# Attention, a dense and a routed MoE layer on one core: late scores with both query parts stacked on the rows

## The chip, the cores and the metric

The kernel runs on one core of a Trainium2 chip. The metric is the device time of one execution in microseconds (us). Before the change, three runs took 986.07, 986.64 and 989.24 us; the median is 986.64.

## The reference

Inputs are fp32. Attention has batch 4, 8 heads, 576 positions and head size 64; the mask works on blocks of 64 positions, so that query block i (0 to 8) sees key blocks 0 to i. Its output feeds a dense layer with a maximum over three products, and that feeds a routed layer with 8 experts, of which each of the 2304 tokens uses 2.

```
scores = scale * q @ k.T ; scores = where(block_i >= block_j, scores, -1e9)
attn = exp(scores - max) ; attn /= attn.sum(-1) + 1e-9 ; out = attn @ v
x = out in rows of 512 (8 heads x 64)
x = max(x @ w1, x @ w2, x @ w3) @ w_out
logits = x @ w_gate + log1p(exp(x @ w_noise)) * noise ; top 2, softmax
out[t] = sum over its 2 experts of weight * (relu(x[t] @ e1[e]) @ e2[e])
```

## The kernel before

**Jobs.** A job is two heads of one batch, and either the early query blocks 0 to 3 or the late ones 4 to 8. There are 32 jobs, 16 of them late. The first eight (early, of batches 0 and 1) run in `start`, whose order for all engines is planned from written costs, due times and dependencies (`add(engine, cost, ...)`) and kept. The other 24 run in a loop behind it, in the order of `MIDDLE`, written by hand: one late job, three early, two late and so on, with ten late jobs in a row at the end. Ten times a late job directly follows a late one. There the scheduler of the tile framework orders each engine's instructions by its own simulation, with the program's order as priority; what the engines execute is that order.

**Between the jobs' steps** the loop calls `gap(j)`, which adds 1.0 us (1.2 us from job 16 on) to a budget and lets the generator `chain` emit as much of the dense layer: units of 256 tokens, in groups of 24 products of 256 columns (L811 to L813), then products of 264 columns (L836 to L840) and the routing (L931 and on). After attention, the rest of the dense layer and the routed layer follow (from 440 us on).

**A late job, exactness.** The scores use fp32r products of a high and a low part: Qh Kh + Ql Kh + Qh Kl. `split_keys` (L284) makes Kh on ScalarE (L288) and Kl = k - Kh on GpSimd (L291), `split_queries` (L293) makes Qh on ScalarE (L298) and Ql on VectorE (L300). The two heads lie on partitions 0 to 63 and 64 to 127. The stationary operand of one query block is block diagonal (128x128, `late_queries` L229 clears the rest), so that one product over 128 rows gives 64 queries of both heads. `prep_job` (L302) does all four for the next late job, right after the scores of the late job before it, since Kh, Kl, Qh and Ql have one buffer each. `load_job` (L271) has by then brought the raw tiles rq and rk, also one buffer each, through SP's queue; the next job's load is issued behind `prep_job`.

**Scores** (`s_block`, L329): for block i, three products with 64 i + 64 columns (L313, L314, L315; block 8 has two halves of 288 columns in tile a2) into one of two PSUM tiles `s`; a maximum on VectorE (L319), an exponential with a row sum on ScalarE (L320) into the tile `PL[i]`, and `scale` (L392: add, reciprocal, multiply on VectorE). `turn_steps` and `score_steps` (L1028 to L1041) pair the transposes of job j with the scores of job j + 1, and a gap stands behind each of five steps:

```
turns  (j):     4 and tail of 8 | 8 | 6 | 7 | 5
scores (j + 1): 4 | 8, scale(4, 8) | 6 | 7, scale(6, 7) | 5, scale(5)
```

**Transposes** (`t_block`, L404; L402) go to PSUM tiles `t` and from there on ScalarE (L416) into the weights tile `PT[j]`, which uses the buffers Ph and Pl in turn. **Values** (`pv`, called behind the scores of the next job): ten fp32 products (L467), a pair for each of five key steps, one head on columns 0 to 63 and one on 64 to 127 of the array. An fp32 product has two records in the trace.

**Memory.** The first eight jobs use four sets of buffers, three of which lie in Qh, Kh, Ph, Ql, Kl, Pl and V. The tiles `PL` also serve the gate's small products in `start` (L569 to L582), by their numbers.

Of the kernel before, what the change touches and what calls it, by code (L numbers as in the profile page):

```python
# [129 lines left out]
def tile_attention_moe_moe(ctx, tc, qT, kT, v, w1, w2, w3, w_out, gates, noise, e1, e2, out):  # L130
    nc = tc.nc
# [70 lines left out]
    PL = {i: att.tile([128, 384 if i == 5 else 128 * (i // 2 + 1)], F32, name=f"p{i}") for i in range(4, 9)}  # L202
    POFF = {3: 0, 2: 256, 0: 512, 1: 640}
    SLOT = {8: 0, 6: 1, 7: 2, 4: 3, 5: 4}

    jp = PL[5][:, :128]
# [11 lines left out]
    LT = {x: n for x, n in (("Qh", 640), ("Ql", 640), ("Kh", S), ("Kl", S), ("V", 1280), ("Ph", 2560), ("Pl", 2560))}  # L218
    t = {x: att.tile([128, n], F32, name=x) for x, n in LT.items()}
    new_set(t["Qh"][:, :512], t["Kh"][:, :512], t["Ph"][:, :768], t["Ph"][:, 768:1536])  # L220
    new_set(t["Ql"][:, :512], t["Kl"][:, :512], t["Ph"][:, 1536:2304], t["Pl"][:, :768])
    new_set(t["V"][:, :512], t["V"][:, 512:1024], t["Pl"][:, 768:1536], t["Pl"][:, 1536:2304])
# [6 lines left out]
    def late_queries(n):  # L229
        QQ.append(att.tile([128, 5, 128], F32R, name=("Qh", "Ql")[n]))  # L230
        nc.gpsimd.memset(plain(QQ[n]), 0.0)

    def late_tails():
        for i in (4, 6, 8):
            nc.gpsimd.memset(PL[i][:, 64 * i + 64:], 0.0)

# [34 lines left out]
    def load_job(j):  # L271
        i = at(j)
        q = att.tile([128, 320], F32, name="rq")
        k = att.tile([128, S], F32, name="rk")
        nc.sync.dma_start(q, qT[i:i + 2, :, 256:S].rearrange("h d n -> (h d) n"))
        nc.sync.dma_start(k, kT[i:i + 2].rearrange("h d n -> (h d) n"))
        RAW[j] = q, k

    def load_values(j):
        n = LJ.index(j) % 2  # L280
        VV[j] = att.tile([128, 1280 if n else 640], F32, name=("rv", "V")[n])[:, :640].rearrange("p (r c) -> p r c", r=2)
        nc.sync.dma_start(VV[j], v[at(j):at(j) + 2].rearrange("h p c d -> p h (c d)"))

    def split_keys(j, low):  # L284
        k = RAW[j][1]
        if not low:
            QK[j] = (att.tile([128, S], F32R, name="Kh"),)
            nc.scalar.activation(QK[j][0], k, AF.Copy)  # L288
        else:
            QK[j] += (att.tile([128, S], F32R, name="Kl"),)  # L290
            nc.gpsimd.tensor_sub(QK[j][1], k, plain(QK[j][0]))  # L291

    def split_queries(j, r, low):  # L293
        m = slice(64 * r, 64 * r + 64)
        src = RAW[j][0][m].rearrange("p (i c) -> p i c", c=64)
        h, l = (x[m, :, m] for x in QQ)
        if not low:
            nc.scalar.activation(h, src, AF.Copy, scale=0.125)  # L298
        else:
            nc.vector.scalar_tensor_tensor(l, src, 0.125, plain(h), op0=OP.mult, op1=OP.subtract)  # L300
# [9 lines left out]
    def scores(ps, j, i, k0, k1):  # L310
        Kh, Kl = QK[j]
        QH, QL = (x[:, i - 4] for x in QQ)
        nc.tensor.matmul(ps, QH, Kh[:, k0:k1], start=True, stop=False)  # L313
        nc.tensor.matmul(ps, QL, Kh[:, k0:k1], start=False, stop=False)  # L314
        nc.tensor.matmul(ps, QH, Kl[:, k0:k1], start=False, stop=True)  # L315
# [11 lines left out]
    SB = {}  # L327

    def s_block(j, i, c):  # L329
        st = new_stats(j)  # L330
        if i == 8:
            ps = psA[0].tile([128, 2, 512], F32, name="a2")
            for r in range(2):
                scores(ps[:, r, 0:288], j, i, 288 * r, 288 * r + 288)
            exps(st, c, ps[:, :, 0:288], PL[8][:, :576].rearrange("p (a b) -> p a b", a=2))
            return
        SB[i] = bank("s")
        ps = SB[i][:, :64 * i + 64]
        scores(ps, j, i, 0, 64 * i + 64)
        exps(st, c, ps, PL[i][:, :64 * i + 64])  # L340

# [50 lines left out]
    def scale(j, c0, blocks):  # L392
        st, z = ST[j][:, 1, c0:c0 + len(blocks)], SB[blocks[0]][:, 500:500 + len(blocks)]
        nc.vector.tensor_scalar(z, st, 1.0e-9, None, op0=OP.add)
        nc.vector.reciprocal(st, z)
        for c, i in enumerate(blocks):
            s = ST[j][:, 1, c0 + c:c0 + c + 1]
            P = PL[i][:, :64 * i + 64]
            nc.vector.tensor_scalar(P, P, s, None, op0=OP.mult)

# [3 lines left out]
    def t_block(j, i, tail=None):  # L404
        if j not in PT:
            PT[j] = att.tile([128, 2, 4, 320], F32, name=("Ph", "Pl")[LJ.index(j) % 2])
        nk = (i + 2) // 2
        if i == 8:
            nk = 4
        ps = bank("t")  # L410
        for key in range(nk):
            turn(ps[:, 128 * key:128 * key + 128], i, key)
        if tail is not None:
            turn(ps[:, 384:512], tail, 4)
        o = 64 * SLOT[i]
        nc.scalar.activation(PT[j][:, :, :nk, o:o + 64].rearrange("p h k c -> p k h c"),  # L416
                             ps[:, :128 * nk].rearrange("p (k h c) -> p k h c", k=nk, h=2), AF.Copy)
        if tail is not None:
# [140 lines left out]
    GT = PL[5][:, 128:192].rearrange("p (k n) -> p k n", k=4)  # L559
# [8 lines left out]
    def gate_copy(g, c):  # L568
        nc.scalar.activation(PL[7 + c][:, :512], GS[g, c], AF.Copy)  # L569
# [888 lines left out]
```

## Time and profile before

| what | us |
|---|---|
| median of three runs | 986.64 |
| the profiled execution | 986.13 |
| its span, from the first to the last instruction | 984.4 |
| PE busy (matmuls) | 971.0 |
| VectorE (DVE) busy | 431.2 |
| ScalarE (ACT) busy | 395.5 |
| GpSimd (POOL) busy | 392.6 |

PE is TensorE. The line numbers are those of the kernel before. A matmul's row gives its start and its duration; matmuls are pipelined, so that the distance from one start to the next is what a product costs PE. "128*64" is the stationary operand: rows by columns of the array. `x20` behind a row says that 20 instructions in a row are merged into it. What ended an idle time is inferred from semaphores.

### The profile page before, as it was taken

Reading aid. Unit: us, or ns where it says so; the run is one execution under the profiler, and the core shown is the slowest. Engines: PE = TensorE matmul, PEld = TensorE weight load, DVE = VectorE, ACT = ScalarE, POOL = GpSimd, SP = SyncE. Lnnn points to the kernel's source line nnn. Section 1 sums busy time; section 2 is a strip of 40 time slices with the busy share of each in tenths; the row PEclk is TensorE's granted clock in tenths of the full one; section 3 lists DMA queues with packets and bytes.
Section 4 is the critical chain, followed back from the end, with each engine's and each line's share of the span. In section 5 each row is a group of like instructions: output and inputs, shape, how many; then the busy total and the mean of one; then the engine's idle time right before and its main releaser. Section 6 shows DMA issues by size and latency. Waiting matters only on the chain. (4 is left out here: it accounts for less than half of the span.)

```text
span 984.4 us, 17147 instructions
## 1 busy us (share of the span) xinstructions
PE 971.0 (99%) x6594; PEld 861.2 (87%) x6594; DVE 431.2 (44%) x1259; ACT 395.5 (40%) x938; POOL 392.6 (40%) x298
## 2 busy tenths in 40 slices
PE   9999999999999999999999999999999999999997
PEld 5856899999898998999999889898988979898895
DVE  7854657654677665632355322222222222221321
ACT  7587545544565555531134234142323323132210
POOL 3595121211213013120221577755836556564302
PEclk9999999999999999999999999999999999999999
DMA  9912414221211312212022546543535354452101
GB/s 322 340 29 71 134 47 155 54 90 31 62 55 36 92 36 68 63 30 85 22 81 82 173 160 196 180 151 108 184 108 162 109 155 146 126 170 77 52 14 57
DMA packets 72550, 106.17 MB, mean 108 GB/s; under 512 B 19196, under 2 KB 44796, under 8 KB 72464
## 3 DMA queue, kind: packets, MB, share of 16 engines
q1 hardware_dynamic: 61120, 75.93, 24.1%
q0 software_dynamic: 10224, 28.32, 8.8%
q8 instruction: 53, 0.87, 0.4%
q10 hardware_dynamic: 1120, 0.79, 0.3%
q14 instruction: 33, 0.27, 0.1%
HBM read 85.35 MB, written 20.53 MB: 108 GB/s over the span
## 5 line engine op out<-in xcount | busy, mean ns | idle before, releaser
L187 POOL TENSOR_TENSOR w<-rw,w 128x1536 fp32r<-128x1536 f32 (+1 forms) x42 | 131.7, 3137 | 71.7 <-ACT w L186 56.2
L827 POOL TENSOR_TENSOR hl<-hm,hh 128x512 fp32r<-128x512 f32 x21 | 27.7, 1317 | 173.3 <-ACT hh L826 173.2
L186 ACT ACTIVATE w<-rw 128x1536 fp32r<-128x1536 f32 (+1 forms) x42 | 56.5, 1345 | 89.2 <-issue 42.1
L1179 PE MATMUL b<-xh,w 128*128 128x384 f32 (+7 forms) x272 | 87.4, 322 | 0.7 <-DVE xB L1184 0.4
L1180 PE MATMUL b<-xl,w 128*128 128x384 f32 (+7 forms) x272 | 87.4, 321 | 0.3 <-DVE xl L1170 0.3
L1181 PE MATMUL b<-xh,w 128*128 128x384 f32 (+7 forms) x272 | 87.6, 322 | 0.0
L811 PE MATMUL t<-xA,w 128*128 128x256 f32 x288 | 83.1, 289 | 0.0
L812 PE MATMUL t<-xA,w 128*128 128x256 f32 x288 | 81.7, 284 | 0.0
L813 PE MATMUL t<-xA,w 128*128 128x256 f32 x288 | 81.5, 283 | 0.0
L1184 DVE SCALAR_TENSOR_TENSOR ht<-b,ht 128x384 fp32r<-128x384 f32 (+6 forms) x56 | 29.1, 520 | 94.3 <-ACT ht L1183 94.3
L1235 POOL DMA_INDIRECT out_rows<-y,isc x37 | 37.5, 1013 | 77.3 <-DVE y L1232 73.1
L1180 PE MATMUL t<-xl,w 128*128 128x256 f32 x240 | 67.3, 280 | 0.0
L1181 PE MATMUL t<-xh,w 128*128 128x256 f32 x240 | 67.3, 280 | 0.0
L1179 PE MATMUL t<-xh,w 128*128 128x256 f32 x240 | 67.3, 281 | 0.0
L1227 PE MATMUL b<-w,ht 128*128 128x512 f32 (+1 forms) x168 | 67.0, 399 | 0.0
L291 POOL TENSOR_TENSOR Kl<-rk,Kh 128x576 fp32r<-128x576 f32 x16 | 23.2, 1450 | 109.0 <-ACT Kh L288 109.0
L1229 PE MATMUL b<-w,ht 128*128 128x512 f32 (+1 forms) x168 | 66.4, 395 | 0.0
L1228 PE MATMUL b<-w,ht 128*128 128x512 f32 (+1 forms) x168 | 66.3, 394 | 0.0
L999 POOL DMA_INDIRECT ids<-rows,slots x36 | 35.9, 996 | 68.4 <-DVE slots L996 60.1
L811 PE MATMUL t<-xB,w 128*128 128x256 f32 x216 | 61.9, 287 | 0.0
L812 PE MATMUL t<-xB,w 128*128 128x256 f32 x216 | 61.3, 284 | 0.0
L813 PE MATMUL t<-xB,w 128*128 128x256 f32 x216 | 61.2, 283 | 0.0
(404 smaller groups left out, 2766.7 us busy)
## 6 DMA issues: line engine op xcount, KB each, us to landing
rw<-in_e SPq DMA_DIRECT2D x32, 768.0 KB, 4.6
w<-in_w SPq DMA_DIRECT2D x18, 512.0 KB, 7.8
rw<-in_e SPq DMA_DIRECT2D x16, 512.0 KB, 3.7
rk<-in_kT SPq DMA_DIRECT2D x16, 288.0 KB, 2.8
x2d<-x SPq DMA_DIRECT2D x18, 256.0 KB, 2.0
out_rows<-x SPq DMA_DIRECT2D x9, 512.0 KB, 3.0
w<-in_w_out SPq DMA_DIRECT2D x6, 512.0 KB, 10.1
rq<-in_qT SPq DMA_DIRECT2D x16, 160.0 KB, 2.3
```

What stands on the lines that cost most here:

```text
L186: nc.scalar.activation(t[:, 0, :c], r[:, :c], AF.Copy)
L187: nc.gpsimd.tensor_sub(t[:, 1, :c], r[:, :c], plain(t[:, 0, :c]))
L811: nc.tensor.matmul(ps[:, j], wh, x[:, 0], start=kt == 0, stop=False)
L812: nc.tensor.matmul(ps[:, j], wh, x[:, 1], start=False, stop=False)
L813: nc.tensor.matmul(ps[:, j], wl, x[:, 0], start=False, stop=kt == 3)
L1179: nc.tensor.matmul(p, wt1(e, 0, kt, f), th[:, kt, c0:c1], start=kt == 0, stop=False)
L1180: nc.tensor.matmul(p, wt1(e, 0, kt, f), tl[:, kt, c0:c1], start=False, stop=False)
L1181: nc.tensor.matmul(p, wt1(e, 1, kt, f), th[:, kt, c0:c1], start=False, stop=kt == 3)
L1227: nc.tensor.matmul(ps, a, wt2(e, 0, f), start=f == 0, stop=False)
L1228: nc.tensor.matmul(ps, a, wt2(e, 1, f), start=False, stop=False)
L1229: nc.tensor.matmul(ps, l, wt2(e, 0, f), start=False, stop=f == 7)
L1235: st = nc.gpsimd.indirect_dma_start(out=out, out_offset=bass.IndirectOffsetOnAxis(ap=at, axis=0), in_=y, in_offset=None, bounds_check=NTOK ...
```

## The change

The late queries are laid out per head. For head r, one operand holds the high part on one half of the rows and the low part on the other (`QQ[r]`), and Kh lies on both halves, so that one product over 128 rows gives Qh Kh + Ql Kh of one head for 128 queries: blocks 4 and 5, or 6 and 7, together. Qh Kl of a head is a product over the 64 rows of the high part. The even block of a pair gets 64 columns of keys too many; they are set to -1e9 in PSUM before the maximum. Block 8 stays one product group for both heads, with the operands padded by zeros and a block-diagonal copy of its high part that GpSimd makes (`block_queries`). A pair takes both `s` tiles, one for each head. The raw queries and keys are loaded on both halves (four DMAs a job instead of two). Scores and transposes have new steps; the weights use Ph alone, and every second job's values lie in Pl.

```diff
-    LT = {x: n for x, n in (("Qh", 640), ("Ql", 640), ("Kh", S), ("Kl", S), ("V", 1280), ("Ph", 2560), ("Pl", 2560))}
+    LT = {x: n for x, n in (("Qh", 512), ("Ql", 384), ("Kh", 2 * S), ("Kl", S), ("V", 768), ("Ph", 2560), ("Pl", 2304))}
...
+        q = att.tile([128, (512, 384)[n]], F32R, name=("Qh", "Ql")[n])
+        QQ.append(q)
+        nc.gpsimd.memset(plain(q[:, 256:320] if n else q[:, 320:]), 0.0)
...
+        q = att.tile([128, 2, 320], F32, name="rq")
+        k = att.tile([128, 2, S], F32, name="rk")
+        for m in HALF:
+            nc.sync.dma_start(q[m], qT[i:i + 2, :, 256:S].rearrange("h d n -> d h n"))
+            nc.sync.dma_start(k[m], kT[i:i + 2].rearrange("h d n -> d h n"))
...
+    HALF = (slice(0, 64), slice(64, 128))
...
-            QK[j] = (att.tile([128, S], F32R, name="Kh"),)
+            QK[j] = (att.tile([128, 2, S], F32R, name="Kh"),)
             nc.scalar.activation(QK[j][0], k, AF.Copy)
         else:
             QK[j] += (att.tile([128, S], F32R, name="Kl"),)
-            nc.gpsimd.tensor_sub(QK[j][1], k, plain(QK[j][0]))
+            for r, m in enumerate(HALF):
+                nc.gpsimd.tensor_sub(QK[j][1][m], k[m, r], plain(QK[j][0][m, r]))
...
     def split_queries(j, r, low):
+        for n, o, w in ((0, 0, 256), (256, 320, 64)) if r else ((0, 0, 320),):
+            q, src = QQ[r][:, o:o + w], RAW[j][0][:, r, n:n + w]
+            if not low:
+                nc.scalar.activation(q, src, AF.Copy, scale=0.125)
+            else:
+                m = HALF[1 - r]
+                nc.vector.scalar_tensor_tensor(q[m], src[m], 0.125, plain(q[m]), op0=OP.mult, op1=OP.subtract)
+
+    def block_queries(r):
+        m = HALF[r]
+        nc.gpsimd.tensor_copy(QQ[0][m, 384 + 64 * r:448 + 64 * r], plain(QQ[r][m, 256 + 64 * r:320 + 64 * r]))
 
     def prep_job(j):
         for low in (False, True):
             split_keys(j, low)
         for r in range(2):
-            for low in (False, True):
-                split_queries(j, r, low)
+            split_queries(j, r, False)
+            block_queries(r)
+            split_queries(j, r, True)
...
+    def s_pair(j, i):
+        Kh, Kl = QK[j]
+        st = new_stats(j)
+        n, c = 64 * i + 128, i // 2 - 1
+        ps = [bank("s") for _ in range(2)]
+        for low in (False, True):
+            for r, m in enumerate(HALF):
+                q = QQ[r][:, 64 * i - 256:64 * i - 128]
+                nc.tensor.matmul(ps[r][:, :n], q[m] if low else q, Kl[m, :n] if low else Kh[:, r, :n],
+                                 start=not low, stop=low)
+        for r in range(2):
+            nc.vector.memset(ps[r][0:64, n - 64:n], -1.0e9)
+            exps(st, 2 * c - 1 + r, ps[r][:, :n], PL[10 * i + r][:, :n])
+        z = ps[0][:, 0:2]
+        scale(j, 2 * c - 1, z, [PL[10 * i + r][:, :n] for r in range(2)])
+
+    def s_eight(j):
...
+        for n in range(3):
+            for x in range(2):
+                k = slice(288 * x, 288 * x + 288)
+                if n < 2:
+                    q, k = QQ[n][:, 256:384], Kh[:, n, k]
+                else:
+                    q, k = QQ[0][:, 384:512], Kl[:, k]
+                nc.tensor.matmul(ps[:, x, 0:288], q, k, start=n == 0, stop=n == 2)
...
+    def t_pair(j, i, r):
+        ps = bank("t")
+        n = i // 2 + 1
+        for key in range(n):
+            turn(ps[:, 128 * key:128 * key + 128], 10 * i + r, key)
...
-            return [lambda: s_block(j, 4, 0), lambda: (s_block(j, 8, 1), scale(j, 0, (4, 8))),
-                    lambda: s_block(j, 6, 2), lambda: (s_block(j, 7, 3), scale(j, 2, (6, 7))),
-                    lambda: (s_block(j, 5, 4), scale(j, 4, (5,)))]
+            return [None, lambda: s_eight(j), lambda: s_pair(j, 4), None, lambda: s_pair(j, 6)]
...
-            return [lambda: t_block(j, 4, 8), lambda: t_block(j, 8), lambda: t_block(j, 6), lambda: t_block(j, 7),
-                    lambda: t_block(j, 5)]
+            return [lambda: t_eight(j), *(lambda i=i, r=r: t_pair(j, i, r) for i in (4, 6) for r in (0, 1))]
```

In `start`, the written costs of the first late job's load and split grow with it (load 0.9 to 1.8 us, Kh 0.68 to 1.2, Kl 1.4 to 2.8), and the two copies of `block_queries` are added to its plan.

## Rows read from the trace of the kernel before

**Rows 1.** The page, busy time, share and instructions of each engine.

```profile
PE 971.0 (99%) x6594; PEld 861.2 (87%) x6594; DVE 431.2 (44%) x1259; ACT 395.5 (40%) x938; POOL 392.6 (40%) x298
```

**Rows 2.** What PE waited for, 95 to 440 us: total us, times, longest.

```profile
PE s L313 <- ACT p L320: 0.6, 2, 0.4
```

**Rows 3.** Busy us of each engine in two stretches; last PE clock, DMA share, GB/s.

```profile
60.00:95.00 35.00, 35.00 (x219) 20.45 (x216) 14.64 (x57) 29.48 (x93) 26.53 (x24) 1.00 0.14 41
380.00:440.00 60.00, 59.74 (x486) 54.66 (x485) 33.40 (x109) 29.68 (x75) 10.74 (x9) 1.00 0.17 46
```

**Rows 4.** Timeline of PE (start, duration), a score group of 512 columns, one of 320.

```profile
330.93 0.39 PE L313 MATMUL s<-Kh,Qh 128*128 128x512 f32 x1
...
331.62 0.28 PE L837 MATMUL t<-w,hh 128*128 128x264 f32 x1
...
339.90 0.31 PE L314 MATMUL s<-Kh,Ql 128*128 128x320 f32 x1
...
340.20 0.28 PE L811 MATMUL t<-xB,w 128*128 128x256 f32 x1
```

**Rows 5.** Timeline of PE, scores of block 5, the value products, MoE products.

```profile
333.66 0.34 PE L314 MATMUL s<-Kh,Ql 128*128 128x384 f32 x1
333.84 0.33 PE L315 MATMUL s<-Kl,Qh 128*128 128x384 f32 x1
334.10 2.28 PE L467 MATMUL t<-Pl,V 128*64 128x320 f32 x20
336.31 0.39 PE L811 MATMUL t<-xB,w 128*128 128x256 f32 x1
336.53 0.28 PE L812 MATMUL t<-xB,w 128*128 128x256 f32 x1
336.65 0.28 PE L813 MATMUL t<-xB,w 128*128 128x256 f32 x1
```

**Rows 6.** Timeline of PE, scores of early jobs on quarters of the array.

```profile
5.85 0.92 PE L358 MATMUL t<-Kh,Qh 64*64 64x256 f32 x8
6.60 0.92 PE L358 MATMUL s<-Kl,Ql 64*64 64x256 f32 x8
```

**Rows 7.** PE's groups by line and shape: busy us and mean ns, idle.

```profile
L608 PE MATMUL t<-hl,w 128*128 128x256 f32 x144 | 31.5, 380 | 0.6 <-POOL w L557 0.6
```

**Rows 8.** Timeline of PE, transposes of a short last tile in the routed layer.

```profile
911.67 0.38 PE L1167 MATMUL t<-ident,xg 128*128 128x128 f32 x2
911.89 0.60 PE L1167 MATMUL b<-ident,xg 128*128 128x128 f32 x4
912.42 0.46 PE L1167 MATMUL t<-ident,xg 64*128 64x64 f32 x4
912.81 0.50 PE L1227 MATMUL b<-w,ht 128*128 128x512 f32 x1
913.15 0.40 PE L1228 MATMUL b<-w,ht 128*128 128x512 f32 x1
```

**Rows 9.** Timeline of all engines, from a late job's last product to the next's first.

```profile
287.40 0.34 PE L315 MATMUL s<-Kl,Qh 128*128 128x384 f32 x1
...
287.65 0.69 ACT L288 ACTIVATE Kh<-rk 128x576 fp32r<-128x576 f32 x1 [0.77 <-PE s L314]
...
288.41 1.42 POOL L291 TENSOR_TENSOR Kl<-rk,Kh 128x576 fp32r<-128x576 f32 x1 [2.87 <-ACT Kh L288]
...
288.72 1.97 DVE L300 SCALAR_TENSOR_TENSOR Ql<-rq,Qh 64x320 fp32r<-64x320 f32 x2 [0.39 <-ACT Qh L298]
...
291.36 0.31 PE L313 MATMUL s<-Kh,Qh 128*128 128x320 f32 x1
...
292.27 0.31 PE L315 MATMUL s<-Kl,Qh 128*128 128x320 f32 x1
```

**Rows 10.** Instructions that write tile Ql: duration ns, least, median, most.

```profile
L300 DVE SCALAR_TENSOR_TENSOR Ql<-rq,Qh x32: 459/490/1611, 74.6 to 405.9; 64x320 fp32r<-64x320 f32 x32
```

More of the change, by code (lines that the diff above doesn't have):

```diff
@@ L199, in tile_attention_moe_moe @@
     before = consts.tile([128, 128], BF, name="before")
-    PL = {i: att.tile([128, 384 if i == 5 else 128 * (i // 2 + 1)], F32, name=f"p{i}") for i in range(4, 9)}
+    PL = {i: att.tile([128, n], F32, name=f"p{i}") for i, n in ((8, 640), (40, 384), (41, 384), (60, 512), (61, 512))}
     POFF = {3: 0, 2: 256, 0: 512, 1: 640}
-    SLOT = {8: 0, 6: 1, 7: 2, 4: 3, 5: 4}
-    jp = PL[5][:, :128]
+    jp = PL[40][:, :128]
     nc.gpsimd.iota(jp, pattern=[[1, 128]], base=0, channel_multiplier=-1,
@@ L325, in new_stats @@
         return ST[j]
-    SB = {}
-    def s_block(j, i, c):
+    def s_pair(j, i):
+        Kh, Kl = QK[j]
         st = new_stats(j)
[L331 to L340, printed above, removed]
+        n, c = 64 * i + 128, i // 2 - 1
[11 more added lines that the diff above has]
+    def s_eight(j):
+        Kh, Kl = QK[j]
+        st = new_stats(j)
+        ps = psA[0].tile([128, 2, 512], F32, name="a2")
+        for n in range(3):
[6 more added lines that the diff above has]
+                nc.tensor.matmul(ps[:, x, 0:288], q, k, start=n == 0, stop=n == 2)
+        exps(st, 0, ps[:, :, 0:288], PL[8][:, :S].rearrange("p (a b) -> p a b", a=2))
+        scale(j, 0, ps[:, 0, 288:289], [PL[8][:, :S]])
     def early_set(j):
@@ L390, in e_scale, with scale @@
                 nc.scalar.activation(P, P, AF.Copy, scale=x)
-    def scale(j, c0, blocks):
-        st, z = ST[j][:, 1, c0:c0 + len(blocks)], SB[blocks[0]][:, 500:500 + len(blocks)]
+    def scale(j, c0, z, blocks):
+        st = ST[j][:, 1, c0:c0 + len(blocks)]
         nc.vector.tensor_scalar(z, st, 1.0e-9, None, op0=OP.add)
         nc.vector.reciprocal(st, z)
[L396 to L399, printed above, removed]
+        for c, P in enumerate(blocks):
+            nc.vector.tensor_scalar(P, P, ST[j][:, 1, c0 + c:c0 + c + 1], None, op0=OP.mult)
@@ L401, in turn, with late_weights, t_eight @@
     def turn(dst, i, key):
         nc.tensor.transpose(dst, PL[i][:, 128 * key:128 * key + 128], ident)
-    def t_block(j, i, tail=None):
+    def late_weights(j):
         if j not in PT:
[L406 to L409, printed above, removed]
+            PT[j] = att.tile([128, 2, 4, 320], F32, name="Ph")
+        return PT[j]
+    def t_eight(j):
         ps = bank("t")
[L411 to L418, printed above, removed]
+        for key in range(4):
+            turn(ps[:, 128 * key:128 * key + 128], 8, key)
+        nc.scalar.activation(late_weights(j)[:, :, :, 0:64].rearrange("p h k c -> p k h c"),
+                             ps.rearrange("p (k h c) -> p k h c", k=4, h=2), AF.Copy)
@@ L1094, in tile_attention_moe_moe @@
                 T[n]()
-            if n < len(SS):
+            if n < len(SS) and SS[n]:
                 SS[n]()
```

60 lines of the change are left out of this document (23 added, 37 removed).

## The prediction

> **What bounds the kernel now.** I read the page's busy shares first: TensorE (PE) is busy 971.0 of 984.4 us [rows 1]. A busy PE need not be a fast one, so I looked at what it waits for while the late attention jobs run, 95 to 440 us: a score group's first product waits for an exponential in two places, 0.6 us together [rows 2]. Then the stretches: from 60 to 95 us PE is busy all 35 us, and from 380 to 440 us it is busy 59.74 of 60 us while VectorE has 33.40, ScalarE 29.68 and GpSimd 10.74 [rows 3]. So time is won here only by giving PE less to do, and lost by anything that makes PE wait: its instructions run in the order that the scheduler wrote, and the MoE work behind a waiting product waits too. I sum against the profiled execution, 986.13 us (span 984.4); the median of the three runs is 986.64, so 0.5 us is added at the end.
>
> **The products.** Each product's price is the distance to the next start, not its duration, because they are pipelined. Three products of 512 columns take 330.93 to 331.62, so 0.23 each; two of 320 take 339.90 to 340.20, so 0.15 each [rows 4]. On the line between these, 384 columns cost 0.18 (333.66 to 333.84 shows that [rows 5]) and 448 cost 0.21. Per late job, blocks 4 to 7 now have twelve products: 3 x (0.15 + 0.18 + 0.21 + 0.23) = 2.31 us. Afterwards the pair of blocks 4 and 5 has two full products of 384 columns, one for each head, and two products that use only 64 rows of the array; the pair 6 and 7 has the same with 512. Block 8 keeps six products of 288 columns: no change. Transposes (19 a job) and the value products keep their sizes.
>
> **Do the two 64-row products run at the same time?** They use different row halves and write different PSUM tiles. No row shows row halves with all 128 columns. The nearest are the quarters of the first jobs: eight records with 1792 columns in all take 5.85 to 6.60, 0.75 us, although an fp32 record of 256 columns costs 31.5/144 = 0.22 us [rows 6, 7], so one after another they would take 1.5 us. The value products, column halves, also overlap: 20 records with 4864 columns would take 4.2 us at that rate and take 2.21 [rows 5, 7]. I take them as overlapped. The bounds: all hidden, or 0.18 + 0.23 = 0.41 us a job more. The Trainium skill (TensorE: Matmul & The Clock Gate, Part 3) says that products in distinct row groups run concurrently, for 64-row tiles too by its mechanism; no run here shows it.
>
> **What a visit to half the array costs.** Going from full products to half ones and back isn't free. After the 384-column product at 333.84, its 0.18 us is over at 334.02, but the value product starts at 334.10, so 0.08 is dead; behind it, the first full product takes 0.22 (336.31 to 336.53) where the next takes 0.12 [rows 5]. The only 64-row products with 128 columns are four transposes of a short tile: two full ones take 0.22, so the four at 911.89 should end at 912.33, but the next starts at 912.42 (0.09 dead); the four 64-wide ones, half a full one each, should take 0.22 and take 0.39 (0.17); the first full product behind takes 0.34 instead of 0.23 (0.11) [rows 8]. Together 0.37 us a visit. The Trainium skill (TensorEngine Tiling (Array Packing), Key Properties) speaks against this change here: changing the tiling mode, not just the tile, drains TensorE; the trace agrees, with 0.08 and 0.09 us dead at the entries. By the rule alone each of the two visits a job costs something; how much, it doesn't say.
>
> So a job costs 3 x 0.18 + 3 x 0.23 + 2 x 0.37 = 1.97 us against 2.31: 0.34 saved, **5.4 us** over 16 jobs. At no price for the visit it would be 17 us; nothing in the rows supports that. At 0.15 us a visit it would be 12.4, at 0.50 it would be 1.3.
>
> **Neighbours.** In five places the value products stand directly behind the last score block, as in [rows 5]. A 64-row pair there would go straight from one half mode to another, and one exit and entry of about 0.2 us falls away: **-1.0**. On the other side the scheduler tears groups: at 291.36 to 292.27 (block 4) the three products were not neighbours: 0.91 us from the first to the third start, where 0.30 would do [rows 9]. A torn pair pays a second visit and the product that was to be hidden, 0.37 + 0.20. I allow for three of 32: **+1.7** (none: 0; twelve: 6.8).
>
> **The preparation.** This is moved work off PE, and it is longer. Today, after the last product of a job (287.40, over at 287.58) ScalarE makes Kh in 0.69 us from 287.65, GpSimd makes Kl in 1.42 from 288.41, VectorE the low queries in 1.97 from 288.72, and the first product that reads Kl starts at 292.27 [rows 9]. Afterwards Kh has twice the columns (at most 1.38 us), Kl is two GpSimd instructions of 576 columns, 1.42 each if the partition count doesn't matter, and two small copies for block 8 stand behind them on GpSimd (64 columns each, a ninth of a Kl: between 0.16 in proportion and the 1.42 of a whole one; I take 0.3, nearer to proportion). Low queries need three instructions in place of two, and every stacked product needs them, where today the first product of each group didn't. Chain: 0.1 + 1.38 + 2 x 1.42 + 0.6 = 4.9 us to the last copy, and 6.1 if VectorE comes to all low queries only then (0.5 + 0.4 + 0.3 more). Room: 4.7 us from the last score to the first read of Kl, and 1.6 more because the first score step moves one step later (one gap of about 1.2 us of MoE work and four transposes at 0.11). So it just fits. Ten jobs follow another late job directly; there I take 0.12 us each: **+1.2** (0 to 7 with 0.7 short each; the other five transitions have an early job between and are covered). If the cover goes, this is what ends late.
>
> **The rest costs PE nothing as long as those engines keep up.** VectorE gets four memsets of 64x64 a job (at the 0.49 of a low query [rows 10], which is five times as wide, under 2 us a job), 128 more columns of maximum and scaling; about four jobs in 60 us then bring it from 33 to at most 44 of 60 us. ScalarE gets under 1 us a job, GpSimd about 2. Two more DMA issues a job stand on SP's queue, and twice the bytes of queries and keys; those loads are issued behind the last reader of the raw tile, now some 2 us later, and are wanted one job, over 10 us, later. Stores behind them on SP slip by as much, and nobody waits for these soon. The score banks: a pair takes both, so pair 6 waits until pair 4's two exponentials are through, but two gaps lie between where today block 5 has one behind block 7 and waits 0.6 us in all [rows 2]; I count zero (-0.6 to +2). At the start the first job's split puts under 2 us more on GpSimd and ScalarE before 95 us, where PE has its own work without a pause [rows 3]: zero, at most +1.4. The value and weight buffers that are merged are reused in the order of the jobs: zero.
>
> **Sum:** -5.4 - 1.0 + 1.7 + 1.2 = -3.5; 986.13 - 3.5 + 0.5 = **983.1**. A measurement of this kernel tells 0.3%, 3.0 us, from no change, so the border to faster is 983.7.
>
> **Rivals.** (1) *The halves don't overlap.* Then 16 x 0.41 = 6.6 us come back, less 0.6 since a tear then loses nothing hidden: 989.1. For it: no row with row halves alone. Against it: quarters and column halves overlap [rows 5, 6]. (2) *Preparation becomes the bound* (the slower end). Place: the ten transitions between late jobs. VectorE's low query took 0.49 us in the median and up to 1.61 [rows 10], and the two of [rows 9] took 1.97 while Kl ran on GpSimd. If with two Kl instructions VectorE waits for both, and the low part of the queries, which now every product reads, comes 0.9 us too late each time, PE loses 9 us: 986.64 - 4.7 + 9 = 990.9. It decides at 0.47 us a transition (no gain left) and 0.77 (slower by 0.3%). For it: the room above is as good as used up. Against it: where the first product was ready early, the scheduler put other work between it and the third [rows 9], so PE need not idle. The Trainium skill (SBUF — State Buffer, Who interferes with whom) has it that a VectorE instruction with two SBUF inputs and a GpSimd instruction that reads SBUF lock each other out for the whole instruction; the trace agrees with the 1.97 us, and by that rule the wait would be one Kl instruction or two, as the issue order has it. (3) *A visit costs 0.15 us*, because the row halves load weights beside each other and ahead: 7 us more gain, 976.1. Against it: 0.37 in the only 64-row rows [rows 8].
>
> **Chances.** Forecast 0.55, reaching from 980 to 986 as tears and waits fall, so some 0.36 of it is faster by over 0.3% and 0.19 within; no overlap 0.13 (0.09 within, 0.04 slower); preparation 0.20 (0.08 within, 0.12 slower); cheap visits 0.12, faster. Faster 0.48, same 0.36, slower 0.16. The range leaves out half of the cheap visits and half of the slow preparation: 978.0 to 989.5.
>
> **What the changed profile would show.** Right: 64-row products of one pair starting within 0.02 us of each other; about 0.2 us more than streaming time on entering and on leaving; the late stretch to 440 us some 3 to 5 us shorter, the rest unchanged. Wrong: the second 64-row product starting 0.18 or 0.23 us behind the first (rival 1); PE idle before the first stacked product of a job, released by VectorE's low queries or GpSimd's Kl or copies (rival 2); many single 64-row products with MoE products between them (more tears than three); PE waiting for pair 6's banks.

## The result and the profile after

The changed kernel takes 1001.16 us (median of 6 runs, 999.46 to 1002.91), the kernel before beside it 986.07: the ratio is 1.015, with a 95% interval of 1.013 to 1.017. It is 15 us slower, where 983.1 was forecast; the range, 978.0 to 989.5, doesn't hold it. The profiled execution took 1002.16 us, span 1000.4.

The page's busy shares (answers to [rows 1]):

```profile
PE 985.9 (99%) x6530; PEld 853.1 (85%) x6530; DVE 448.4 (45%) x1339; ACT 402.4 (40%) x954; POOL 423.4 (42%) x344
```

TensorE executes 64 products fewer and is busy 14.9 us more. PE's waits from 95 to 440 us (answers to [rows 2]), first the longest one of the kernel before, which [rows 2] leaves out, then the two longest after:

```profile
PE s L355 <- ACT pe L390: 1.7, 1, 1.7
...
PE s L336 <- ACT p L321: 1.8, 1, 1.8
PE a L355 <- DVE Qh L303: 0.7, 1, 0.7
```

All waits of this stretch make 3.7 us before and 3.2 after, so the 15 us are not waiting. Three stretches (columns as in [rows 3]):

```profile
60.00:95.00 35.00, 34.35 (x201) 18.08 (x198) 15.54 (x49) 29.10 (x91) 23.50 (x23) 1.00 0.07 23
380.00:440.00 60.00, 60.00 (x445) 50.47 (x446) 38.31 (x129) 31.29 (x80) 16.79 (x18) 1.00 0.24 69
...
110.00:113.00 3.00, 3.00 (x12) 2.12 (x12) 2.88 (x8) 2.83 (x6) 2.23 (x3) 0.51 0.91 294
```

From 380 to 440 us PE has no pause and starts 445 products where it started 486; the change itself takes away 4 a job, some 16 here. So PE is not kept waiting there; its products follow each other at longer distances. From 110 to 113 us the granted clock is 0.51, the lower level.

I split the time at two starts: the first product of unit 1 of the dense layer, and the last product of that layer's first step. Up to the first is the **front** (before 151.71 us, after 156.40: 4.7 us longer), between them lies the **steady stretch** with some 14 of the 16 late jobs (before 359.04, after 368.99: 9.9 longer). Behind them 1.4 us of the profiled executions' difference are left; at the entry to the routed layer PE waits 1.1 us for VectorE, 0.4 before. No run was made for these.

PE's timeline (start, duration), a pair of blocks 6 and 7 issued as it was drawn up, which I call whole:

```profile
275.83 0.48 PE L336 MATMUL s<-Kh,Qh 128*128 128x512 f32 x1
276.15 0.40 PE L336 MATMUL s<-Kh,Ql 128*128 128x512 f32 x1
276.48 0.49 PE L336 MATMUL s<-Kl,Qh 64*128 64x512 f32 x1
276.48 0.49 PE L336 MATMUL s<-Kl,Ql 64*128 64x512 f32 x1
276.90 0.65 PE L489 MATMUL t<-pte,kve 128*64 128x256 f32 x4
```

and one as 11 of the 16 pairs of blocks 6 and 7 ran:

```profile
361.31 0.40 PE L336 MATMUL s<-Kh,Qh 128*128 128x512 f32 x1
361.64 0.49 PE L336 MATMUL s<-Kl,Qh 64*128 64x512 f32 x1
362.06 0.39 PE L836 MATMUL t<-xB,w 128*128 128x256 f32 x1
362.28 0.28 PE L834 MATMUL t<-xB,w 128*128 128x256 f32 x1
362.40 0.28 PE L835 MATMUL t<-xB,w 128*128 128x256 f32 x1
362.52 0.40 PE L336 MATMUL s<-Kh,Ql 128*128 128x512 f32 x1
362.84 0.50 PE L336 MATMUL s<-Kl,Ql 64*128 64x512 f32 x1
363.27 0.38 PE L836 MATMUL t<-xB,w 128*128 128x256 f32 x1
363.50 0.28 PE L834 MATMUL t<-xB,w 128*128 128x256 f32 x1
```

In the first group the two halves run at once (both start at 276.48). In the second, head 0 goes alone, then dense work, then head 1: the pair is torn, its two 64-row products are no neighbours. So it is with 16 of 32 pairs (5 of them of blocks 4 and 5). The whole pair costs 1.07 us plus its exit; each torn head costs 0.75 and an exit of 0.22 - 0.12 = 0.10, both together 1.70.

The value products (answers to [rows 5]), a torn group and a whole one:

```profile
343.43 0.75 PE L489 MATMUL t<-Ph,V 128*64 128x320 f32 x2
344.11 0.39 PE L834 MATMUL t<-xB,w 128*128 128x256 f32 x1
...
348.04 2.27 PE L489 MATMUL t<-Ph,V 128*64 128x320 f32 x18
350.24 0.39 PE L836 MATMUL t<-xB,w 128*128 128x256 f32 x1
...
365.39 2.28 PE L489 MATMUL t<-Ph,Pl 128*64 128x320 f32 x20
367.60 0.39 PE L834 MATMUL t<-xB,w 128*128 128x256 f32 x1
```

Head 0's first product (two records) went alone and takes 0.68 us, and the other 18 records still take 2.20, as long as all 20 together (2.21). The two heads do overlap among these 18, their first records start 7 ns apart; but head 1 still has all its ten, 2432 columns, which at 0.22 us for 256 [rows 7] are 2.1 us by themselves, an estimate. So what was to be hidden in head 0's lone product is simply added. So it is in 11 of 16 jobs. In the steady stretch the distances from start to start, summed by function, rise by 6.60 us for the values, 2.07 for the late jobs' transposes and 4.65 for the dense products (exits are counted with the product behind them), and fall by 2.82 for blocks 4 to 7.

The timeline of all engines behind the first stretch of [rows 3], where the first late job begins:

```profile
91.14 0.37 ACT L599 ACTIVATE p<-t 16x256 f32<-16x256 f32 x1 [3.25 <-PE t L655]
...
92.18 6.25 POOL L619 TENSOR_TENSOR w<-xB,w 128x512 fp32r<-128x512 f32 x5 [1.87 <-ACT w L621]
...
95.94 1.27 DVE L955 TENSOR_SCALAR rt<-rt 128x16 f32<-128x16 f32 x1 [2.39 <-ACT rt L954]
...
106.75 1.02 DVE L320 TENSOR_REDUCE st<-s 128x1 f32<-128x384 f32 x2
...
108.63 0.49 PE L336 MATMUL s<-Kh,Qh 128*128 128x512 f32 x1 [1.85 <-ACT p L321]
```

`start` is planned from written costs, and with the larger ones of the preparation ScalarE's queue has the logit rows (L599) ahead of the splits of w_out (L621) into xB, where before four of these stood ahead of them. The rows wait 3.25 us for PE, and what stands behind them on ScalarE comes late: GpSimd's operands, and the routing's first step, for which VectorE waits 2.39 us (95.94; before, its routing started at 92.34). The maxima of the first late job are late behind it, PE waits 1.85 us, and then its clock is at the lower level. That each of these steps causes the next is read from the rows; that the order as a whole costs time is tested below (`s1_start_order`).

### The profile page after: what moved, and what is told of

It is laid out like the page before. It is cut to its first block, busy times and chain, and to the rows that moved or that the text cites. A ratio compares the mean times of both kernels' runs of the same rounds, so it can differ in the third digit from the quotient of the medians.

```text
span 1000.4 us, 17279 instructions
## 1 busy us (share of the span) xinstructions
PE 985.9 (99%) x6530; PEld 853.1 (85%) x6530; DVE 448.4 (45%) x1339; ACT 402.4 (40%) x954; POOL 423.4 (42%) x344
## 5 line engine op out<-in xcount | busy, mean ns | idle before, releaser
L834 PE MATMUL t<-xA,w 128*128 128x256 f32 x288 | 84.0, 292 | 0.0
L835 PE MATMUL t<-xA,w 128*128 128x256 f32 x288 | 82.6, 287 | 0.0
L836 PE MATMUL t<-xA,w 128*128 128x256 f32 x288 | 82.5, 287 | 0.0
L294 POOL TENSOR_TENSOR Kl<-rk,Kh 64x576 fp32r<-64x576 f32 x32 | 47.3, 1478 | 41.9 <-ACT Kh L290 40.1
```

Of the source, the lines that this page charges most:

```text
L294: nc.gpsimd.tensor_sub(QK[j][1][m], k[m, r], plain(QK[j][0][m, r]))
L834: nc.tensor.matmul(ps[:, j], wh, x[:, 0], start=kt == 0, stop=False)
L835: nc.tensor.matmul(ps[:, j], wh, x[:, 1], start=False, stop=False)
L836: nc.tensor.matmul(ps[:, j], wl, x[:, 0], start=False, stop=kt == 3)
```

## The experiments

Steady and front are the stretches above, in the profiled execution. The column "torn" counts pairs of 32, then groups of values of 16 in which head 0 starts alone; "-" stands where there are no pairs.

| run | median us | ratio [95%] | torn | front | steady |
|---|---|---|---|---|---|
| before | 986.07 | 1 | - | 151.71 | 359.04 |
| after | 1001.16 | 1.0150 [1.013, 1.017] | 16, 11 | 156.40 | 368.99 |
| e1_weights_by_key | 991.15 | 1.0052 [1.0032, 1.0072] | 15, 0 | 156.27 | 358.68 |
| e2_two_bank_tile | 1023.69 | 1.0385 [1.0367, 1.0402] | 0, 12 | 170.01 | 377.15 |
| e3_full_rows | 993.21 | 1.0073 [1.0056, 1.009] | no half rows, 13 | 159.31 | 357.11 |
| q7_before_half_rows | 1003.71 | one run | - | 151.70 | 376.49 |
| e12_two_of_two_banks | 1003.05 | 1.0173 [1.0149, 1.0198] | 0, 9 | 162.46 | 363.70 |
| e9_both_untorn | 996.42 | 1.0108 [1.0079, 1.0136] | 0, 0 | 161.56 | 357.02 |
| e4_full_rows_by_key | 989.32 | 1.0026 [1.0012, 1.0039] | no half rows, 0 | 166.31 | 347.73 |
| e10_full_rows_untorn | 993.76 | 1.0069 [1.0049, 1.0089] | no half rows, 0 | 168.76 | 349.74 |
| s1_start_order | 998.28 | 1.0126 [1.011, 1.0142] | 16, 11 | 152.77 | 369.14 |
| s2_start_order_by_key | 988.48 | 1.0024 [1.0015, 1.0034] | 15, 0 | 154.80 | 358.68 |
| s3_start_order_full_rows_by_key | **978.22** | 0.9919 [0.9906, 0.9932] | no half rows, 0 | 154.20 | 348.84 |
| s4_start_order_by_key_untorn | 998.24 | 1.0119 [1.0102, 1.0135] | 0, 0 | 164.48 | 358.06 |
| m1_pairs_in_order | 993.65 | 1.0078 [1.0065, 1.0091] | 2, 11 | 155.41 | 362.85 |
| m2_pairs_and_values_in_order | 988.31 | 1.0029 [1.0017, 1.0041] | 1, 0 | 157.68 | 352.37 |
| m3_pairs_values_start_in_order | 986.88 | 1.0006 [0.9997, 1.0014] | 1, 0 | 159.35 | 352.63 |
| m4_key_halves_pairs_start | 986.60 | 1.0016 [1.0005, 1.0027] | 1, 0 | 157.74 | 352.12 |
| g1_m4_more_dense_work_first | 986.64 | 1.0005 [0.9996, 1.0015] | 0, 0 | moved | moved |
| g2_s3_more_dense_work_first | 979.14 | 0.9932 [0.9919, 0.9945] | no half rows, 0 | moved | moved |

**Copies by key halves.** The weights of blocks 6 and 7 are copied for both heads at once.

```diff
+    def t_six(j, key):
+        ps = bank("t")
+        for r in range(2):
+            for k in range(2):
+                turn(ps[:, 256 * r + 128 * k:256 * r + 128 * k + 128], 60 + r, key + k)
+        nc.scalar.activation(late_weights(j)[:, :, key:key + 2, 64:192],
+                             ps.rearrange("p (r k c) -> p r k c", r=2, k=2), AF.Copy)
...
-            return [lambda: t_eight(j), *(lambda i=i, r=r: t_pair(j, i, r) for i in (4, 6) for r in (0, 1))]
+            return [lambda: t_eight(j), *(lambda r=r: t_pair(j, 4, r) for r in (0, 1)),
+                    lambda: t_six(j, 2), lambda: t_six(j, 0)]
```

> The changed kernel, but the weights of blocks 6 and 7 are turned and copied two key tiles at a time for both heads (keys 2 and 3 first), so that the value products of both heads become ready together. Visits theory (PE loses its time in entering and leaving half of the array, 0.37 us a visit, because pairs and value products are torn): the static order has 14 visits fewer and the 11 value groups with one product of head 0 alone in front cost 2.2 instead of 2.88 us, so 7.5 us less than the changed kernel, about 993.5. Preparation theory (all score products wait for the longer chain of Kh, Kl and low queries): nothing in that chain changes, within 1.5 us of 1001.

The run takes 10.0 us fewer than the changed kernel, and no group of values is torn; the values' distances in the steady stretch sum to 36.90 us again (before 37.05, after 43.65). The visits theory named 993.5 and was nearer than its rival.

**A two-bank tile for a pair.** One PSUM tile holds both heads of a pair, also of an early job.

```diff
+    def both():
+        return psA[0].tile([128, 2, 512], F32, name="s2")
...
-        ps = [bank("s") for _ in range(2)]
+        two = both()
+        ps = [two[:, r] for r in range(2)]
```

> The changed kernel, but both heads' scores of a pair (and of an early job) share one PSUM tile of two banks, which is given free as a whole; the order then has no torn pair (16 of 32 before), the value products stay torn. Visits theory: about 12 visits fewer (4.6 us) and 16 products of 0.18 or 0.23 us hidden again (3.4 us), so 8 us less, about 993; each pair's two 64-row products start within 0.02 us. Preparation theory: no gain, rather a loss of 1 to 3 us, since the first head's scores now wait for the second bank: 1001 to 1004.

Both theories miss, by 19 us and more. No pair is torn, but with one such tile PE stands still; its longest waits:

```profile
PE s L341 <- DVE st L423: 6.6, 2, 4.8
PE s L341 <- DVE st L409: 4.0, 2, 2.5
PE s L383 <- DMA qe<-in_qT: 2.9, 1, 2.9
```

**Two of them**, shared by block 8, the pairs and the early jobs, with the copies of the change, then with key halves:

> The changed kernel, but all scores (block 8, pairs, early jobs) take turns on two PSUM tiles of two banks each, in place of two of one bank and one of two. No pair is torn in the order, and a pair no longer waits for the pair before it, as it did when one such tile served them all. Visits theory, with the price of the half-row run (0.15 us a change between whole and half array): 39 changes fewer (5.9 us) and 16 products hidden again (3.4 us), 2 us of PE idle at the first late job gone: 990. Waiting theory (a tile that is given free as a whole costs waits in itself): over 1003, as the run with one such tile.

> Both repairs on the changed kernel: weights of blocks 6 and 7 by key, and two score tiles of two banks. Neither pairs nor value products are torn: 105 changes against 136 with the weights by key alone. Visits theory: 4.7 us for the changes, 3.2 for hidden products, 2 for the idle time less than 991.2, so 981 to 984, below the kernel before, near what the prediction had for untorn pairs. If half-array products lose by themselves: 988 or more.

Both are over 12 us above what the visits theory named, and in the range of its rival: waits for the shared tiles stand in place of the tears. PE's waits of the second, 60 to 155 us:

```profile
PE a L383 <- DMA kve<-in_kT: 2.3, 1, 2.3
PE a L341 <- DVE st L409: 2.2, 1, 2.2
PE a L341 <- DVE cum L1006: 2.2, 1, 2.2
```

So runs with these tiles don't measure what a tear costs.

**The visit alone, in the kernel before:** the Kl product of blocks 4 to 7 reads 64 rows and leaves out the second head's low part.

```diff
-        nc.tensor.matmul(ps, QH, Kl[:, k0:k1], start=False, stop=True)
+        m = slice(0, 128 if i == 8 else 64)
+        nc.tensor.matmul(ps, QH[m], Kl[m, k0:k1], start=False, stop=True)
```

> The kernel before, but the product with Kl of blocks 4 to 7 reads only rows 0 to 63 (the low part of the second head's keys is left out). Streaming, order and preparation stay; 64 visits to a row half are added. Visits theory at 0.37 us each: 64 x 0.37 = 24 us, less some 2 us where the value products follow directly: 1007 to 1010. If a visit to a row half is cheap, as 0.15 us, 995; if free, 986.

PE's timeline, one group:

```profile
341.74 0.39 PE L313 MATMUL s<-Kh,Qh 128*128 128x512 f32 x1
341.97 0.40 PE L314 MATMUL s<-Kh,Ql 128*128 128x512 f32 x1
342.29 0.49 PE L316 MATMUL s<-Kl,Qh 64*128 64x512 f32 x1
342.72 0.39 PE L838 MATMUL t<-w,hh 128*128 128x264 f32 x1
342.95 0.28 PE L837 MATMUL t<-w,hh 128*128 128x264 f32 x1
343.06 0.28 PE L838 MATMUL t<-w,hh 128*128 128x264 f32 x1
```

The single run took 1003.71, between the theory's price (1007 to 1010) and the cheap visit (995). A 512-column product costs 0.23; here 0.09 is lost on entering, 0.20 behind the half product and 0.11 in the product after: 0.40. The steady stretch, with 56 of the 64 visits, is 17.45 us longer (376.49 against 359.04), 0.31 each on the mean; 14 of these go straight on to the values' column halves. The front with the other eight is as long as before (151.70), so there they cost nothing. The Trainium skill (TensorEngine Tiling (Array Packing), Key Properties) states that a change of tiling mode drains TensorE; the trace agrees, with the 0.09 and 0.20 us around the half product.

**Full rows for the low product**, with a zero-padded copy of the high part, with the copies of the change and then with key halves:

```diff
-                q = QQ[r][:, 64 * i - 256:64 * i - 128]
-                nc.tensor.matmul(ps[r][:, :n], q[m] if low else q, Kl[m, :n] if low else Kh[:, r, :n],
+                q = (QZ[0][:, r] if low else QQ[r])[:, 64 * i - 256:64 * i - 128]
+                nc.tensor.matmul(ps[r][:, :n], q, Kl[:, :n] if low else Kh[:, r, :n],
```

> The changed kernel, but the products with Kl use all 128 rows: the high part of the queries is copied once more with zeros on the other half of the rows. No score product visits half the array, none is hidden behind another. Visits theory: 43 visits fewer (15.9 us), 16 products come out of hiding (3.3 us): 12.6 us less, about 988.5, although two more ScalarE instructions stand in the preparation. Preparation theory: the chain is longer by 0.8 us, so no gain, 1001 or more.

> Weights of blocks 6 and 7 by key, and the products with Kl on all 128 rows with zeros in the other half: 50 changes, fewer than the kernel before (54); score tiles as in the changed kernel, so pairs are torn, which costs nothing here. Visits theory: against the weights by key alone 86 changes fewer (13.1 us), 17 products out of hiding (3.5 us): 981.6, and up to 3 more if the longer start stays. Preparation theory: two ScalarE instructions more in the chain, 990 or more.

The first stays 4.7 us above the visits theory's figure. The second, 989.32, is 7.7 us above it and near the rival's 990, but not for the rival's reason: its steady stretch is 11.3 us shorter than before, so the stacking works there, and the front is 14.6 longer. PE's longest wait in the front, and the stretch from 104 to 111 us with its clock:

```profile
PE t L849 <- ACT hm L854: 6.1, 2, 5.3
```
```profile
104.00:111.00 7.00, 1.73 (x10) 1.41 (x9) 6.68 (x25) 0.84 (x3) 3.94 (x5) 0.81 0.63 170
```

With the two-bank tiles on top:

> All three: weights by key, full rows, two score tiles of two banks. As the run with full rows and weights by key, since tears cost nothing where no product visits half the array: within 2 us of it; 979 if the idle time at the first late job goes too.

This is 4.4 us worse than without them, where within 2 us was expected; the other kernels got slower by such tiles too.

**The start's order.** The plan is told the old costs; the work stays. Four runs: the changed kernel, with key halves, with full rows and key halves, and with key halves and the two-bank tiles:

```diff
-        x = add("SP", 1.8, lambda: load_job(first), [LD[23], gt], 3.0, late=2.0, load=3.0)
+        x = add("SP", 0.9, lambda: load_job(first), [LD[23], gt], 3.0, late=2.0, load=1.5)
...
-        a = add("ACT", 1.2, lambda: split_keys(first, False), [x, EV[4]], 3.0)
-        add("POOL", 2.8, lambda: split_keys(first, True), [a, EV[5]], 3.0)
+        a = add("ACT", 0.68, lambda: split_keys(first, False), [x, EV[4]], 3.0)
+        add("POOL", 1.4, lambda: split_keys(first, True), [a, EV[5]], 3.0)
...
```

> The changed kernel; alone the start's planner is told the durations of before for the first late job's preparation (loads 0.9 and 1.5, key copies 0.68 and 1.4, query copies 0.47 and 0.5, block 8's copies next to nothing, both zero fills as one step). The work is the same; in ScalarE's order five of the w_out splits stand ahead of the logit rows again, as before, and in the steady stretch nothing is different (164 changes, 16 torn pairs). Theory: 4.7 us of the 15 come from the start's order, by VectorE's late routing and maxima and TensorE's half clock behind them; the first moe1 product of unit 1 comes 4 us sooner and the kernel at 997 us. Rival: what the start loses is the doubled preparation itself (Kl 2.8 and Kh 1.2 us in place of 1.4 and 0.68), which is still there: within 1 us of 1001.

> The start's order of before, with the weights of blocks 6 and 7 turned and copied by key halves for both heads (991.15 us alone). Theory of two separate losses that add: 987 us, steady stretch as in the run by key halves (359 us from unit 1's first hidden product to the last one). Rival, preparation itself: 991.

> The start's order of before with the full-row low products and the weights by key halves (989.32 us alone, of which the steady stretch took 347.7 us, 11.3 less than before, and the stretch up to unit 1's first hidden product 166.3, 14.6 more than before). Theory: most of the 14.6 goes back, 977 us (975 to 980), faster than the kernel before. Rival, that the front's loss is the work of the preparation (two more copies of the queries here) or of GpSimd's late splits in whatever order: 986 or more.

> The change as it was pictured before it ran: the start's order of before, the weights of blocks 6 and 7 by key halves, and two two-bank tiles for block 8, the pairs and the early jobs, so that all 32 pairs are issued whole (105 changes of the array, where the run with start order and key halves alone has 136 and took 988.48 us). In the run with these tiles and the start's new order the steady stretch from unit 1's first hidden product to the last took 357.0 us, 1.7 less than with 15 torn pairs, and the front stretch 161.6. Theory that a visit to the half rows costs nearly as much whole as torn, and that the front's loss went with the start's order: 985 to 988 us, no faster than the kernel before. Rival, that torn pairs are what costs and whole visits are cheap: 979 to 982, near the run with full rows (978.22). Third, that early jobs and pairs wait for each other at the shared tiles in the front whatever the start's order: 991 to 995.

In the first three 2.9, 2.7 and 11.1 us go back against the same kernels with the new start. The timeline of the first, the same rows as above of the changed kernel:

```profile
89.38 0.36 ACT L599 ACTIVATE p<-t 16x256 f32<-16x256 f32 x1
...
89.91 6.26 POOL L619 TENSOR_TENSOR w<-xB,w 128x512 fp32r<-128x512 f32 x5
...
92.46 1.25 DVE L955 TENSOR_SCALAR rt<-rt 128x16 f32<-128x16 f32 x1
```

These rows stand 1.8 to 3.5 us earlier, the wait is 1.2 us in place of 1.8, and the clock from 95 to 125 us is 1.00 in place of 0.94. The third run beats both kernels, by 0.8% over the one before. The fourth misses all three of its theories: its front is 164.48 us, as with the other shared tiles, whatever the start's order.

**The order alone.** The scheduler keeps the four products of a pair as written; then also the value products, head 1 first, as its weights come last; then with the start's old costs.

```diff
+        with tc.manual_schedule(engines={PE}):
+            for low in (False, True):
+                for r, m in enumerate(HALF):
...
-            for r in range(2):
+            for r in heads:
...
+        with tc.manual_schedule(engines={PE}):
+            values(p, ((0, 0, 320, (0, 0)), (1, 0, 320, (1, 0)), (2, 0, 320, (2, 0)), (3, 0, 192, (3, 0)), (4, 0, 64, (3, 192))),
+                   VV.pop(j), lambda r, o, w: t[:, r, o[0], o[1]:o[1] + w], (1, 0))
```

> The changed kernel; the scheduler is told to keep the four products of a pair in the written order on TensorE (both full products, then both 64-row ones). Same tiles, same work: 30 of 32 pairs whole in place of 16, 137 changes between whole and half array in place of 164; the value products stay torn. Theory that torn pairs cost as the timeline reads, some 0.55 us each for a second entry and exit and for the product no longer hidden: 14 x 0.55 = 7.7 us, 993 us. Rival, from the runs with shared two-bank tiles, that whole pairs wait for the second bank as long as a torn one loses: 999 or more.

> The run before with the ten value products of a late job also kept in written order, head 1 first (its weights are copied last), so that no head starts alone; the per-head copies of the weights stay as in the change. 108 changes. Theory: the values go back from 2.88 to 2.2 us in 11 of 16 groups and one visit each falls away, as copies by key halves did: 10 us less than the run with pairs in order, 983 us. Rival, that the gain of the key halves came from the copies and not from the order: within 2 us of the run with pairs in order.

> All three put back at once with none of the work changed: pairs and values in order, and the start planned with the durations of before. This is the change as it was pictured before it ran. Theory, that these three are the whole of the miss: 2.9 us less than the run with pairs and values in order, 980 us (978 to 984), the forecast's 983.1 or better. Rival, that something else of the change costs: 987 or more.

The first decides what a tear costs: 7.5 us for 14 pairs, 0.54 each, without any other edit (in the profiled executions front and steady stretch together are 7.1 us shorter). The second wins 10.5 us in the steady stretch, where its theory had 10 in all, but 5.3 in all: the front grows by 2.3 us, and at the entry to the routed layer PE now waits, with a clock of 0.89 from 530 to 545 us:

```profile
PE b L1203 <- DVE xB L1208: 1.9, 1, 1.9
```

The third ends at 986.88, not 980: no faster than the kernel before (ratio 1.0006). Its PE timeline shows one place in the front:

```profile
121.61 3.22 PE L492 MATMUL t<-Ph,Pl 128*64 128x320 f32 x20 [2.82 <-ACT Ph L442]
```

The first late job's values wait for their last weights. Three runs were to settle that: key halves in place of the forced order of the values, then more dense work ahead of that job's values (`gap(j)` three times), and the same in the fastest kernel.

```diff
+        if j == first:
+            gap(j)
+            gap(j)
+            gap(j)
         pv(j)
```

> The change with the start planned by the durations of before, the weights of blocks 6 and 7 copied by key halves for both heads (988.48 us so far) and the four products of a pair kept in written order: no torn value products without a forced order that makes the first late job wait 2.8 us for its last weights, as the run with all three in order did (986.88). 108 changes, one torn pair. Theory: the steady stretch from unit 1's first hidden product to the last falls from 358.7 to 352.5 us by the whole pairs and the front stays at 154.8: 982.3 us (981 to 984), where the forecast stood. Rival, that what the pairs win is lost again in front of the first late job's second pair: 986 or more.

> The run with key halves, pairs in order and the start of before (986.6 us), with three more gaps of dense work in front of the first late job's value products, and only there: 48 of the first layer's products stand between its last transposes and its values, where 24 stood ahead of the transposes and none behind. Theory that the change's last loss lies at this one place, where TensorE waited 3.4 us for the last copied weights and ran at half clock behind it, while the steady stretch (352.1 us) already has the gain that was forecast: 982 us (981 to 984). Rival, that the front is short of work as a whole and the wait moves to a later place: 985 or more.

> The same three gaps in the run with full-row low products, key halves and the start of before (978.22 us), where the first late job's value products came without that wait. Theory, that the gaps take a wait away and have no worth of their own: 977 to 979. Rival, that they shorten the front by themselves: 976 or less.

The first two ended where their rivals had them, at 986.60 and 986.64. In the first the same wait is there (3.4 us); in the second it is 0.5 us, and others, 60 to 220 us, have taken its place:

```profile
PE s L339 <- ACT p L321: 2.2, 2, 1.2
PE s L375 <- ACT hh L860: 1.7, 1, 1.7
PE t L846 <- DVE xA L517: 1.2, 1, 1.2
```

The third (979.14, against 978.22 without it) shows that the edit has no worth of its own. So the wait moves when it is taken away at one place; that the front is short of work as a whole, with too little dense work ready, is argued, not shown.

## Why the prediction was wrong

**What held.** PE is the bound: an edit of nothing but products' shapes (`q7_before_half_rows`) or order (`m1_pairs_in_order`) moves the time by what their distances sum to. The halves overlap (3 to 4 ns between their starts in every whole pair of the changed kernel), so the first rival falls. A visit was put at 0.37 us; the timeline shows 0.40 and the mean of the steady stretch is 0.31. A torn pair was put at 0.57 more; it is 0.54. "Products" and "neighbours" were to give 6.4 us in 16 jobs, 0.40 a job; with whole pairs and values the steady stretch is 6.4 to 6.9 us shorter than before over 14 jobs, 0.46 to 0.49 a job. The third rival (a visit at 0.15) falls with the same numbers.

**The step that failed first: "I allow for three of 32".** It was 16, and the runs give 7.5 us for 14. The one group of [rows 9] that I called torn wasn't counted over the trace: in the kernel before 10 of 64 score groups were torn, as often as 5 of 32. Why the change makes it 16 stays open. A whole pair needs two banks and two operands at once. In 5 of the 16 torn pairs a tile `s` was still in use for earlier scores when head 0 began, so a bank may have parted them. In the other 11 the last such use had ended 0.6 to 4.1 us before head 0 began, so on the chip no bank held head 1 back. In the torn pair above, which starts at 361.31, that use was this:

```profile
359.20 0.17 DVE L412 RECIPROCAL st<-s 128x2 f32<-128x2 f32 x1
```

There the tear is in the order that the scheduler wrote; what in its simulation parts the heads isn't on record.

**Second: "the value products keep their sizes".** They did, but not their order. I priced the buffers of the weights and never asked which head's copy ends last. This is worth 9.8 to 10.0 us by key halves, and by order alone 10.5 us in the steady stretch but 5.3 in all.

**Third: "At the start ... zero, at most +1.4".** I asked whether GpSimd and ScalarE had room, and did not see that a plan made from other written costs is another plan. This is worth 2.9 us, and 11.1 in the kernel with the queries' extra copy.

Taken one by one, 8.6 (16 tears at 0.54), 9.8 and 2.9 make 21.3, less the 1.7 allowed: 983.1 + 19.6 = 1002.7, against 1001.16. That this comes so close is in part luck: undone together, the three give back only 14.3 us (`m3_pairs_values_start_in_order`) or 14.6 (`m4_key_halves_pairs_start`).

**The second rival (preparation)** doesn't explain it: in the steady stretch PE waits for VectorE's queries once, 0.7 us (and 1.1 us in the front of `m3` and `m4`). In the timeline of one of the ten transitions (answers to [rows 9]) both Kl copies are over at 351.33 and the first product that reads Kl starts at 355.44:

```profile
347.04 1.17 ACT L290 ACTIVATE Kh<-rk 128x1152 fp32r<-128x1152 f32 x1
...
348.29 3.04 POOL L294 TENSOR_TENSOR Kl<-rk,Kh 64x576 fp32r<-64x576 f32 x2 [1.09 <-ACT Kh L290]
...
355.44 0.43 PE L355 MATMUL a<-Kl,Qh 128*128 128x288 f32 x2
```

So the 1.2 us I added for it don't show.

**What stays open.** With all three put back the kernel takes 986.6 to 986.9, 3.5 to 3.8 us over the forecast, though its steady stretch is as good as forecast: the front, 6.0 to 7.6 us longer than before, takes the gain back. From 60 to 160 us PE waits 6.7 and 6.9 us there, 2.9 before. Repairs add up in the steady stretch and not in the whole.

## What to carry to other kernels

A packed pair is worth its price only if both parts are issued together: before counting on one, count in the trace how often such neighbours are parted today, over all of it and not at one place, and ask which instruction makes each part's operands ready last. Where an order is worked out by a scheduler or a plan, a change of shapes or costs is a change of order; the first thing to compare is how many products changed their neighbour. And zero-padding to the full array, which streams one product more a pair but makes no visit, was the better form of this change: 978.22 us.

## What the hardware showed that was not expected

- Half rows won nothing over full rows: in the steady stretch the products of blocks 4 to 7 take 27.0 to 27.5 us as whole pairs on half rows (`m2` to `m4`) and 26.2 as four full products with zeros (`s3`; before: 36.1), and the exits of the half rows come on top.
- Column halves that lose step by one product still run at once: 18 records took 2.20 us, where their 4224 columns one after another would take 3.6, an estimate at the 0.22 us for 256 of [rows 7]. What is lost is the product that went alone.
- A GpSimd subtraction over 64 partitions takes as long as over 128: 3.04 / 2 = 1.52 us here, 1.42 in [rows 9].
- While GpSimd subtracts, VectorE's tensor_scalar of 128x16 takes 1.21 to 1.27 us, about one GpSimd instruction (6.25 / 5 = 1.25); other VectorE operations of that size take 0.17 to 0.18 once it is done. The Trainium skill (SBUF — State Buffer, Who interferes with whom) counts tensor_scalar among the operations that can take the ports VectorE shares with GpSimd, with one locking the other out; the durations agree.
- A pause of PE of 1.85 us was followed by some 3 us at the lower clock level (0.51 granted, 110 to 113 us). In the kernel before a pause of 1.67 us in the same stretch (before 117.57 us) was not: there the granted clock is 1.00.
